# Phi of q in the buffer of phi of k, a first norm tile by tile, a second norm in two parts, and a column-tiled form for the values of segment 1: one change to a scheduled two-layer kernel

## The chip, the cores and the metric

One core of a Trainium2 chip. The metric is device time in microseconds (us) of one execution; the kernel before takes 573.08 us (median of 3, from 572.8 to 573.13). Profiles give a span that is some 1.8 us shorter than the time of the same execution, since it starts with the first instruction.

The engines are called PE or TensorE (matmul), PEld (its weight loads, which overlap its matmuls), DVE (VectorE), ACT (ScalarE), POOL (GpSimd) and SP (here the queue that issues DMA). PSUM is the memory that this kernel's matmuls write, and from which ACT or DVE copies on.

## The reference

Two layers, each an attention block with a memory and a feed-forward block (FFN), both on normed input:

```python
x = x + attn(layernorm(x))      # layer 1; 2048 tokens of 640, 32 heads of 20
x = x + relu(layernorm(x) @ w1) @ w2        # 640 -> 1728 -> 640
x = x + attn(layernorm(x))      # layer 2, the same weights
x = x + relu(layernorm(x) @ w1) @ w2

def attn(x):                    # cut to what matters
    for s in range(4):          # four segments of 512 tokens
        qs, ks, vs = ...        # 512 x 20 for each head
        a_dot = softmax(qs @ ks.T * scale + causal_mask) @ vs
        a_mem = (phi(qs) @ M) / (phi(qs) @ z + 1e-6)    # phi(t) = t+1 if t>0 else exp(t)
        outs.append(g * a_mem + (1 - g) * a_dot)
        M = M + phi(ks).T @ vs
        z = z + phi(ks).sum()
    return concat(outs) @ wo
```

## The kernel before

The file does not list instructions in their order. Each piece of work is a generator ("stream"), and a list scheduler with a small model of the engines walks all streams and appends, step by step, the operation that could start first. What comes out is a fixed order of instructions on each engine, with semaphore waits. Constants of the model never reach the chip: they only decide the order, and which of ACT and DVE does a copy out of PSUM that either could do.

```python
SEM_NS = 60.0
BY_TOKEN = 2 * G                # G = 8 groups of 4 heads in a segment
...
class Sched:
    def run(self):
        while True:
            ...                 # let every stream come to its next operation
            for prio, n, st, alts, op, late in heads:
                ...             # start = max(engine free, each awaited one + SEM_NS)
                key = (round(start + late), 0.5 if op.urgent else prio, self.rank[id(st[1])], n)
                if best is None or key < best[0]:
                    best = (key, st, end, start, k, op)
            ...                 # append it to its engine's list, advance the model
```

Values (`p @ v`) come in two forms. For the first 16 groups, segments 0 and 1 of layer 1, "by token": 40 small matmuls with tokens on the output's partitions, ready to be divided. Later groups use a column-tiled form: 16 wide matmuls, four at a time on quarters of the array; the result is transposed, so it is copied to SBUF, turned by a DMA transpose, pair by pair, and divided then.

```python
def apply(n):
    ...
    if n < BY_TOKEN:
        yield from apply_by_token(n, a, s, g, pt, mk + vt)
        return
    ...
    OD, tk = yield pe(540.0, fns, mk + vt, acq=MISC, mode="cols", lag=COLS_LAG)
    te = yield evac(L, 1, ...)          # to otu, on ACT or DVE; then turn_pair, divide
```

The norm of a segment: statistics of four tiles on DVE, one power on POOL, four normed tiles, two DMA transposes. The FFN's first matmuls need all four tiles.

```python
def lnorm(s, x_tks, pool_, parts=1):
    n = 4 // parts
    for p0 in range(0, 4, n):
        for i in range(p0, p0 + n):
            tk = yield from stats(4 * s + i, w)                 # bn_stats twice, bn_aggr
        tch = yield from chain(4 * s + p0, n, aggr)             # lnU on DVE, power on POOL
        for i in range(p0, p0 + n, 2):
            ...                                                 # two normed tiles (DVE)
            tT = yield from turn(xn_sem[id(bx)], xt.ap[...], bx.ap, [t0, t1] + xt.tks)

def ln_b(a, s):                         # the norm ahead of the FFN
    xt, xtk = yield from lnorm(s, xa, XNT_B)
```

phi of k goes to a buffer `phs`, from which a DMA transpose turns it; phi of q overwrites q in its slot, which stays taken until the read of the memory:

```python
    q = STGS[sx(a, s)][:, c, n, :]
    dst, dw = (phs[:, c * L:(c + 1) * L], PHS[c // 3].tks) if n == 0 else (q, [])
```

The softmax here doesn't subtract the row's maximum and nothing guards it: scores larger than these inputs give would overflow.

## Time and profile before

573.08 us. The page of the profile, parts 1 (busy time and share of each engine), 2 (the span in 40 slices, busy tenths) and 4 (shares of the chain of waits that ended last):

```profile
PE 558.2 (98%) x5442; PEld 306.3 (54%) x5442; DVE 406.4 (71%) x1056; ACT 408.3 (72%) x519; POOL 186.3 (33%) x291
...
PE   7999999999999999999999999999999999999998
...
PEclk9999999999999999999999999999999999999999
...
PE 82%; DVE 9%; DMA 3%; ACT 3%; SPq 1%; issue 0%; POOL 0%
```

PE is busy nearly everywhere, and 82% of the chain of waits is its. But a matmul's record is longer than its turn (0.38 us for 512 columns, where the next one can start after 0.216 us), so "busy" hides waiting. The Trainium skill ("Perfetto Trace Analysis", the note at its head) calls matmul busy time a bad metric because matmuls are pipelined.

Start, from the timeline (start, duration, engine, line, operation, output<-input, and in brackets the idle time before it and what ended it):

```profile
7.45 0.17 DVE L708 TENSOR_SCALAR mv<-asum 128x2 f32<-128x2 f32 x1 [1.67 <-ACT hT L705]
7.52 0.80 DVE L655 TENSOR_SCALAR xn_tok<-x_sb,mv,rstd 128x640 bf16<-128x640 bf16 x2
...
10.08 0.27 PE L590 MATMUL ps<-xnT,wk_r 128*128 128x256 bf16 x1 [1.25 <-ACT xnT L685]
...
19.96 1.94 ACT L1113 ACTIVATE PT<-ps 128x1024 bf16<-128x1024 f32 x2 [1.69 <-PE ps L1051]
```

DVE waited 1.67 us for ACT ahead of the norm; the first projection is at 10.08 us, the first exponential at 19.96.

Busy time by stage (the stretch, its length, then busy us and instructions of PE, PEld, DVE, ACT, POOL; granted PE clock, DMA share, GB/s):

```profile
core 0: us, PE busy (x) PEld busy (x) DVE busy (x) ACT busy (x) POOL busy (x), PEclk, DMA share, GB/s
40.00:80.00 40.00, 37.17 (x527) 19.68 (x524) 36.72 (x96) 38.39 (x46) 20.44 (x31) 1.00 0.87 201
80.00:100.00 20.00, 20.00 (x257) 11.29 (x255) 19.45 (x58) 17.50 (x23) 7.89 (x12) 1.00 0.75 143
```

In 40 to 80 us ACT is busy 38.4 of 40 us and DVE 36.7: PE depends on them there.

The two forms of values in PE's timeline:

```profile
90.18 1.17 PE L1184 MATMUL ps<-v_aug,PT 128*128 128x21 bf16 x40
91.20 0.81 PE L593 MATMUL ps<-hT,wk_r 128*128 128x512 bf16 x3
...
133.94 0.72 PE L1145 MATMUL ps<-PT,v_aug 128*21 128x512 bf16 x16
134.60 0.31 PE L593 MATMUL ps<-wo_r,oT 128*128 128x320 bf16 x1
```

By token, the next matmul starts 1.02 us later; column-tiled, 0.66 us later.

The output of segment 0 of layer 1 is turned (on SP) for the output projection, and some time later the first FFN matmul runs:

```profile
70.98 3.05 SPq L621 DMA_TRANSPOSE oT<-o_sb  x2
```

```profile
100.27 0.38 PE L590 MATMUL ps<-xnT,w_r 128*128 128x512 bf16 x1
```

### The profile page before, as it was taken

Reading aid. Unit: us, or ns where it says so; the run is one execution under the profiler, and the core shown is the slowest. Engines: PE = TensorE matmul, PEld = TensorE weight load, DVE = VectorE, ACT = ScalarE, POOL = GpSimd, SP = SyncE. Lnnn points to the kernel's source line nnn. Section 1 sums busy time; section 2 is a strip of 40 time slices with the busy share of each in tenths; the row PEclk is TensorE's granted clock in tenths of the full one; section 3 lists DMA queues with packets and bytes.
Section 4 is the critical chain, followed back from the end, with each engine's and each line's share of the span. In section 5 each row is a group of like instructions: output and inputs, shape, how many; then the busy total and the mean of one; then the engine's idle time right before and its main releaser. Section 6 shows DMA issues by size and latency. Waiting matters only on the chain.

```text
span 571.0 us, 13253 instructions
## 1 busy us (share of the span) xinstructions
PE 558.2 (98%) x5442; PEld 306.3 (54%) x5442; DVE 406.4 (71%) x1056; ACT 408.3 (72%) x519; POOL 186.3 (33%) x291
## 2 busy tenths in 40 slices
PE   7999999999999999999999999999999999999998
PEld 6664555455555543663446544465445643665655
DVE  4768999998889787879577996689747864561202
ACT  5599998987896778878768788777867778213140
POOL 4236434343434343434313443034421533100000
PEclk9999999999999999999999999999999999999999
DMA  8587997573461715843159131791419411423101
GB/s 265 89 222 163 228 186 133 156 202 57 86 171 45 111 20 153 161 66 62 23 148 185 30 65 38 179 145 22 77 42 193 109 42 20 93 65 43 51 0 47
DMA packets 125741, 59.90 MB, mean 105 GB/s; under 512 B 104562, under 2 KB 115570, under 8 KB 125682
## 3 DMA queue, kind: packets, MB, share of 16 engines
q1 hardware_dynamic: 125552, 58.90, 47.5%
q8 instruction: 43, 0.70, 0.5%
q10 hardware_dynamic: 130, 0.16, 0.2%
q14 instruction: 16, 0.13, 0.1%
HBM read 20.57 MB, written 12.85 MB: 59 GB/s over the span
## 4 chain that ended last, share of the span: by engine, by line
PE 82%; DVE 9%; DMA 3%; ACT 3%; SPq 1%; issue 0%; POOL 0%
PE ps L593 53%; PE ps L590 11%; PE ps L1051 8%; PE ps L1145 5%; PE ps L1184 2%; ACT PT L1113 2%; DVE stats L601 2%; PE ps L943 1%; PE ps L994 1%; DVE xn_tok L643 1%; DMA beta_bc<-in_A_beta_dram 1%; DVE x_sb L1267 1%; PE ps L1318 1%; DMA hT<-xn_tok 1%; DMA oT<-o_sb 1%; DVE o_sb L1239 1%
## 5 line engine op out<-in xcount | busy, mean ns | idle before, releaser
L1113 ACT ACTIVATE PT<-ps 128x1024 bf16<-128x1024 f32 x320 | 309.2, 1024 | 68.5 <-PE ps L1051 67.6
L1125 POOL TENSOR_SCALAR_AFFINE_SELECT PT<-PT 128x512 bf16<-128x512 bf16 x256 | 164.9, 662 | 282.3 <-ACT PT L1113 282.3
L593 PE MATMUL ps<-w_r,hT 128*128 128x320 bf16 x768 | 121.8, 299 | 0.0
L593 PE MATMUL ps<-xnT,w_r 128*128 128x512 bf16 x416 | 115.4, 379 | 0.0
L1267 DVE TENSOR_TENSOR x_sb<-x_sb,ps 128x320 bf16<-128x320 bf16 x128 | 60.3, 479 | 74.6 <-PE ps L593 74.2
L593 PEld LDWEIGHTS ps<-w_r,hT 128*128 128x128 bf16 x768 | 73.7, 98 | 31.2 <-issue 3.5
L1051 PE MATMUL ps<-pad 20*128 20x512 bf16 (+3 forms) x1024 | 63.4, 301 | 1.3 <-ACT PT L1113 0.9
L593 PEld LDWEIGHTS ps<-xnT,w_r 128*128 128x128 bf16 x416 | 39.7, 98 | 43.7 <-issue 4.7
L1345 ACT ACTIVATE hT<-ps 128x512 bf16<-128x512 f32 x55 | 32.9, 599 | 33.7 <-PE ps L593 33.6
L601 DVE BATCH_NORM_STATS2 stats<-x_sb 128x6 f32<-128x320 bf16 x124 | 55.6, 472 | 1.8 <-DMA x_sb<-in_A_x_dram 1.5
L593 PE MATMUL ps<-wo_r,oT 128*128 128x320 bf16 x256 | 46.5, 299 | 0.0
L1051 PEld LDWEIGHTS ps<-pad 20*128 20x128 bf16 x1024 | 17.8, 92 | 49.2 <-ACT PT L1113 23.1
L1343 DVE TENSOR_SCALAR hT<-ps 128x512 bf16<-128x512 f32 x49 | 33.2, 681 | 14.2 <-PE ps L593 14.2
L766 DVE CAST stg<-ps 128x512 bf16<-128x512 f32 (+1 forms) x45 | 28.4, 630 | 20.2 <-PE ps L593 20.1
L590 PE MATMUL ps<-xnT,w_r 128*128 128x512 bf16 x104 | 39.6, 381 | 0.0
L593 PE MATMUL ps<-wv_r,xnT 128*128 128x320 bf16 x192 | 36.1, 299 | 0.0
L1155 DVE CAST otu<-ps 128x512 bf16<-128x512 f32 x39 | 26.7, 684 | 12.3 <-PE ps L1145 12.0
L593 PE MATMUL ps<-xnT,wk_r 128*128 128x512 bf16 (+1 forms) x140 | 35.1, 349 | 0.0
L1145 PE MATMUL ps<-PT,v_aug 128*21 128x512 bf16 (+3 forms) x768 | 34.7, 301 | 0.2 <-DVE hT L1343 0.2
L593 PE MATMUL ps<-xnT,wq_r 128*128 128x512 bf16 (+1 forms) x140 | 33.8, 349 | 0.0
L911 ACT ACTIVATE stg<-stg 128x512 bf16<-128x512 bf16 x50 | 30.6, 630 | 3.0 <-DVE rtmp L909 2.9
L643 DVE TENSOR_SCALAR xn_tok<-x_sb,mv,rstd 128x640 bf16<-128x640 bf16 x60 | 30.1, 536 | 2.7 <-POOL rstd L615 2.7
(112 smaller groups left out, 685.1 us busy)
## 6 DMA issues: line engine op xcount, KB each, us to landing
pad<-scr SPq DMA_DIRECT2D x124, 80.0 KB
scr<-stg SPq DMA_DIRECT2D x34, 256.0 KB, 2.6
out_dram<-x_sb SPq DMA_DIRECT2D x16, 160.0 KB, 1.8
w_r<-in_B_w_dram SPq DMA_DIRECT2D x10, 216.0 KB, 4.5
w_r<-in_B_w_dram SPq DMA_DIRECT2D x13, 160.0 KB, 2.9
x_sb<-in_A_x_dram SPq DMA_DIRECT2D x10, 160.0 KB, 2.3
scr<-w_r SPq DMA_DIRECT2D x5, 256.0 KB, 3.9
x_sb<-in_A_x_dram SPq DMA_DIRECT2D x3, 320.0 KB, 7.3
```

What stands on the lines that cost most here:

```text
L590: bk, tk = yield pe(mm_ns(n), [(lambda e, bk, a=a, b=b: e.matmul(bk.ap[:, 0:n] if len(b.shape) == 2 else bk.ap[:, 0:n].rearrange("p (i n) ...
L593: tk = yield pe(mm_ns(n), [(lambda e, k=k, a=a, b=b, bk=bk: e.matmul(bk.ap[:, 0:n] if len(b.shape) == 2 else bk.ap[:, 0:n].rearrange("p (i ...
L601: tk = yield dve(320, 1, lambda e, c2=c2: e.bn_stats(stats6[:, t % 12, c2, :], x_sb[:, t, c2 * 320:(c2 + 1) * 320]), xt)
L643: nm = lambda e, bx, t, k: e.tensor_scalar(bx.ap[:, k * D:k * D + D], x_sb[:, t + k, :], mv[:, t + k, 0:1], rstd[:, t + k:t + k + 1], ALU. ...
L911: te = yield act(512, lambda e, q=q: e.activation(q, q, ACT.Exp), [tr] + p, psum=False)
L1051: fns.append([(lambda e, z=z, j=j, hh=hh, N=N, o=o, sl=sl, q=hh % 2: e.matmul(slot.ap[:, q, o:o + N], sl.ap[32 * hh:32 * hh + DH, z, 0, 12 ...
L1113: tx = yield act(1024, lambda e, dst=dst, src=src: e.activation(dst, src, ACT.Exp, scale=SCALE), sc + pw)
L1125: tm = yield pool(600.0, lambda e, reg=reg: e.affine_select(out=reg, in_=reg, pattern=[[0, 4], [1, 128]], compare_op=ALU.is_ge, fill=0.0, ...
L1145: fns.append((lambda e, OD, j=j, hh=hh: e.matmul(OD.ap[32 * hh:32 * hh + DH + 1, 128 * j:L], VAUG[vx(a, s)][:, j, 4 * g + hh, :], pt.ap[:, ...
L1267: ta = yield dve(320, 1, lambda e: e.tensor_tensor(x_sb[:, t, 320 * hf:320 * hf + 320], x_sb[:, t, 320 * hf:320 * hf + 320], bk.ap[:, 0:32 ...
L1343: th = yield evac(512, 1, lambda e, dc=dc, bk=bk: e.tensor_scalar(hT[:, dc, :], bk.ap[:, :], 0.0, None, ALU.max), lambda e, dc=dc, bk=bk: ...
L1345: lambda e, dc=dc, bk=bk: e.activation(hT[:, dc, :], bk.ap[:, :], ACT.Relu), [tk] + HT.tks)
```

## The change

Its intent, part by part: get the first projection out sooner (four loads, statistics and power tile by tile, the mean on ACT); spend less PE time on the values of segment 1 (column form from group 8 instead of 16); free the slots of q sooner (phi of q to `phs` too); hold the norms of segments 2 and 3 back so that DVE can empty PSUM; turn the first half of the second norm while the second half is still in its statistics; load FFN weights at another pace; and let stores be a stream of their own. The scheduler's model also gets a rule that holds certain DVE instructions back while POOL is at work, and some other estimates of durations. The diff, cut to its core (cuts marked):

```diff
-BY_TOKEN = 2 * G
+BY_TOKEN = G
 ...
+            if e == "dve" and op.port and self.free["pool"] > start:
+                hold = max(hold, self.free["pool"] - start + PORT_NS)
 ...
-            for t in range(2):
-                yield from ld("sp", "x00%d" % t, 163840, lambda e, t=t: e.dma_start(x_sb[:, t, :], xs[:, t, :]))
-            yield from x_pair("x01", 2)
+            for t in range(4):
+                yield from ld(("sp", "act")[t // 2], "x0%d%d" % divmod(t, 2), 163840, lambda e, t=t: e.dma_start(
+                    x_sb[:, t, :], xs[:, t, :]))
 ...                                   # consts: most memsets, and so the load of beta, after the first norm
+            yield Need("xt", 0, 0, 1)
 ...
-            tk = yield pe(5000.0, [... k == 59) for k in range(60)], idt)
+            tk = yield pe(4600.0, [... k == 51) for k in range(52)], idt)
 ...
+            if n == 1:
+                tk = yield pool(150, lambda e: e.tensor_scalar(lnU[:, sl], mv[:, sl, 1], 1.0, LN_EPS, ALU.mult, ALU.add), tk)
 ...                                   # first_pair -> first_sums, first_one, first_tile
-            tm = yield dve(2, 1, lambda e: e.tensor_scalar(
-                mv[:, 2:4, 0:1], asum[:, 0:2][:, :, None], 1.0 / D, None, ALU.mult), ts)
+            tm = yield act(100, lambda e: e.activation(
+                mv[:, 2:4, 0:1], asum[:, 0:2][:, :, None], ACT.Copy, scale=1.0 / D), ts, psum=False)
 ...
+            if (a, s) == (0, 2):
+                yield Need("sc",2,3,1)
+            if (a, s) == (0, 3):
+                yield Need("sc",3,4,1)
 ...
-                    if n == 0 and c in (0, 3):
+                    if c in (0, 3):
+                        if n == 0 and (s > 1 or (a, s) == (1, 0)):
+                            yield Need("phi", *divmod(NSEG * a + s - 1, NSEG))
+                        if n == 1:
+                            yield Need("turned", a, s, c // 3)
                         yield Acq([PHS[c // 3]])
-                    dst, dw = (phs[:, c * L:(c + 1) * L], PHS[c // 3].tks) if n == 0 else (q, [])
+                    dst, dw = phs[:, c * L:(c + 1) * L], PHS[c // 3].tks
 ...
-            xt, xtk = yield from lnorm(s, xa, XNT_B)
+            xt, xtk = yield from lnorm(s, xa, XNT_B, parts=2)
 ...                                   # stores, weight loads in halves, streams
```

More of the change, by code (lines that the diff above doesn't have):

```diff
@@ L110, with __init__ @@
 class Op:
-    def __init__(self, alts, waits, dma=None, acq=None, urgent=False, take=(), mode="full", lag=0.0):
+    def __init__(self, alts, waits, dma=None, acq=None, urgent=False, take=(), mode="full", lag=0.0, port=False):
         self.lag = lag
+        self.port = port
         self.alts = alts
@@ L290, in run @@
                 raise RuntimeError("stuck: " + "; ".join(
-                    str(getattr(st[2], "key", None) or [s.name for s in st[2].slots][:2]) for st in stuck))
+                    str(getattr(st[2], "key", None) or [s.name for s in getattr(st[2], "slots", [])][:2]) for st in stuck))
             _, st, end, start, k, op = best
@@ L329, in mm_ns, with dve @@
     return max(26.0, n / 2.4 + 2.6)
-def dve(n, mode, fn, waits=(), extra=0.0, acq=None, urgent=False):
-    return Op([("dve", 66.0 + n / (0.96 * mode) + extra, [(fn, True)], 95.0)], waits, acq=acq, urgent=urgent)
+PORT_NS = 150.0
+def dve(n, mode, fn, waits=(), extra=0.0, acq=None, urgent=False, port=False):
+    return Op([("dve", 66.0 + n / (0.96 * mode) + extra, [(fn, True)], 95.0)], waits, acq=acq, urgent=urgent,
+              port=port or mode > 1)
 def act(n, fn, waits=(), psum=True):
-    return Op([("act", (52.0 if psum else 94.0) + n / 1.2, [(fn, True)], 125.0)], waits)
+    return Op([("act", (60.0 if psum else 94.0) + n / 1.2, [(fn, True)], 125.0)], waits)
 def evac(n, mode, vfn, afn, waits=(), psum=True):
-    return Op([("act", (52.0 if psum else 94.0) + n / 1.2, [(afn, True)], 125.0),
+    return Op([("act", (60.0 if psum else 94.0) + n / 1.2, [(afn, True)], 125.0),
                ("dve", 66.0 + n / (0.96 * mode), [(vfn, True)], 95.0)], waits, urgent=True)
@@ L449, in ld @@
         def ld(e, name, nbytes, fn, waits=()):
-            tk = yield dma(e, sem_("d_" + name), nbytes, fn, waits, lat=2200.0)
+            tk = yield dma(e, sem_("d_" + name), nbytes, fn, waits, lat=1550.0 if name[:2] == "x0" else 2000.0)
             S.set(name, tks=[tk])
@@ L489, in half @@
                 cs = slice(h * (DFF // 2), (h + 1) * (DFF // 2))
-                return ("w1", 221184, lambda e: e.dma_start(w1_r[:, k, cs], B_w1[128 * k:128 * k + 128, cs]))
+                return ("w1%d" % h, 221184, lambda e: e.dma_start(w1_r[:, k, cs], B_w1[128 * k:128 * k + 128, cs]))
             pieces = x_pieces(2)
@@ L494, in late_loads @@
             pieces += x_pieces(3)
-            pieces += [half(k, h) for k in range(FC) for h in range(2)]
+            pieces += [half(k, h) for h in range(2) for k in range(FC)]
             n2 = len(pieces)
@@ L507, in late_loads @@
                     sems[name] = sem_("d_" + name)
-                w = yield Need("ex", *divmod(n, 5))
+                w = yield Need("ex", *divmod(25 + (n - n2) // 2 if n >= n2 else n * 19 // n2, 5))
                 if n == n2:
@@ L518, in consts @@
         def consts():
+            tw = yield dve(4, 1, lambda e: e.memset(warm[:], 0.0))
+            yield act(4, lambda e: e.activation(warm[:], warm[:], ACT.Exp), [tw], psum=False)
+            t0 = yield pool(150, lambda e: e.memset(ident[:], 0.0))
+            t1 = yield pool(250, lambda e: e.affine_select(
+                out=ident[:], in_=ident[:], compare_op=ALU.not_equal, fill=1.0, base=0,
+                pattern=[[-1, 128]], channel_multiplier=1), [t0])
+            S.set("ident", tks=[t1])
+            th = yield pool(100, lambda e: e.memset(mhalf[:], -0.5))
+            S.set("mhalf", tks=[th])
+            yield Need("xt", 0, 0, 1)
             tv = []
@@ L529, in consts @@
             S.set("z1", tks=[za, zb])
-            ta = yield dve(4, 1, lambda e: e.memset(warm[:], 0.0))
-            yield act(4, lambda e: e.activation(warm[:], warm[:], ACT.Exp), [ta], psum=False)
-            t0 = yield pool(150, lambda e: e.memset(ident[:], 0.0))
-            t1 = yield pool(250, lambda e: e.affine_select(
-                out=ident[:], in_=ident[:], compare_op=ALU.not_equal, fill=1.0, base=0,
-                pattern=[[-1, 128]], channel_multiplier=1), [t0])
-            S.set("ident", tks=[t1])
-            th = yield pool(100, lambda e: e.memset(mhalf[:], -0.5))
-            S.set("mhalf", tks=[th])
             t3 = yield pool(700, lambda e: e.memset(maskg[:], 1.0))
@@ L574, in warm_pe @@
             yield Acq([X])
-            tk = yield pe(5000.0, [(lambda e: e.matmul(
-                ps[:, 0, 0:128], ident[:], ident[:], start=True, stop=True), k == 59) for k in range(60)], idt)
+            tk = yield pe(4600.0, [(lambda e: e.matmul(
+                ps[:, 0, 0:128], ident[:], ident[:], start=True, stop=True), k == 51) for k in range(52)], idt)
             X.release(tk)
@@ L602, in stats @@
                     stats6[:, t % 12, c2, :], x_sb[:, t, c2 * 320:(c2 + 1) * 320]), xt)
-            tk = yield dve(12, 1, lambda e: e.bn_aggr(
+            tk = yield dve(50, 1, lambda e: e.bn_aggr(
                 mv[:, t, :], stats6[:, t % 12, :, :].rearrange("p c s -> p (c s)")), [tk])
@@ L609, in chain @@
             sl = slice(t0, t0 + n)
-            if sq is None:
-                tk = yield dve(n, 1, lambda e: e.tensor_scalar(lnU[:, sl], mv[:, sl, 1], LN_EPS, None, ALU.add), tk)
+            if n == 1:
+                tk = yield pool(150, lambda e: e.tensor_scalar(lnU[:, sl], mv[:, sl, 1], 1.0, LN_EPS, ALU.mult, ALU.add), tk)
+            elif sq is None:
+                tk = yield dve(n, 1, lambda e: e.tensor_scalar(lnU[:, sl], mv[:, sl, 1], LN_EPS, None, ALU.add), tk, port=True)
             else:
@@ L614, in chain @@
             h = yield Need("mhalf")
-            tk = yield pool(1000, lambda e: e.tensor_tensor(rstd[:, sl], lnU[:, sl], mhalf[:, 0:n], ALU.pow), [tk] + h)
+            tk = yield pool(740, lambda e: e.tensor_tensor(rstd[:, sl], lnU[:, sl], mhalf[:, 0:n], ALU.pow), [tk] + h)
             return tk
@@ L657, in normed @@
                 ALU.subtract, ALU.mult), [tch], extra=120)
-        def first_pair(p, tch):
-            idt = yield Need("ident")
-            if p == 0:
-                xt = yield Acq(XNT_A)
-                xt.users = []
-                S.set("xts", 0, 0, tks=[xt])
-            else:
-                xt = yield Need("xts", 0, 0)
-                xt = xt[0]
-            bx = yield Acq(XN)
-            done = []
-            tns = []
-            for k in range(2):
-                tn = yield normed(2 * p + k, k, bx, tch)
-                tns.append(tn)
-            for k in range(2):
-                t = 2 * p + k
-                tn = tns[k]
-                pb = lambda bk: bk.ap.bitcast(dt.bfloat16)
-                fns = [(lambda e, bk, c=c, k=k: e.transpose(
-                    pb(bk)[:, c * 128:(c + 1) * 128], bx.ap[:, k * D + c * 128:k * D + c * 128 + 128], ident[:]),
-                    c == FC - 1) for c in range(FC)]
-                bk, tT = yield pe(56.0 * FC, fns, [tn] + idt, acq=MISC)
-                dst = xt.ap[:, t * FC:(t + 1) * FC, :].rearrange("p c n -> p (c n)")
-                src = pb(bk)[:, 0:D]
-                tc = yield evac(D, 1, lambda e, dst=dst, src=src: e.tensor_copy(dst, src),
-                                lambda e, dst=dst, src=src: e.activation(dst, src, ACT.Copy), [tT])
-                bk.release(tc)
-                done.append(tc)
-            bx.release(tT)
-            S.set("xt", 0, 0, p, tks=done)
@@ L691, in first_ln_a, with first_tile @@
-        def first_ln_a():
-            aggr = []
+        def first_tile(t, bx, tch):
+            xt = yield Need("xts", 0, 0)
+            xt = xt[0]
+            k = t % 2
+            tn = yield normed(t, k, bx, tch)
+            idt = yield Need("ident")
+            pb = lambda bk: bk.ap.bitcast(dt.bfloat16)
+            fns = [(lambda e, bk, c=c: e.transpose(
+                pb(bk)[:, c * 128:(c + 1) * 128], bx.ap[:, k * D + c * 128:k * D + c * 128 + 128], ident[:]),
+                c == FC - 1) for c in range(FC)]
+            bk, tT = yield pe(56.0 * FC, fns, [tn] + idt, acq=MISC)
+            dst = xt.ap[:, t * FC:(t + 1) * FC, :].rearrange("p c n -> p (c n)")
+            src = pb(bk)[:, 0:D]
+            if t < 2:
+                tc = yield dve(D, 2, lambda e: e.tensor_copy(dst, src), [tT])
+            else:
+                tc = yield evac(D, 2, lambda e: e.tensor_copy(dst, src), lambda e: e.activation(dst, src, ACT.Copy), [tT])
+            bk.release(tc)
+            FIRST.setdefault(t // 2, []).append((tc, tT))
+            if len(FIRST[t // 2]) == 2:
+                bx.release(*[x for _, x in FIRST[t // 2]])
+                S.set("xt", 0, 0, t // 2, tks=[x for x, _ in FIRST[t // 2]])
@@ L693, in first_ln_a, with first_sums @@
+        FIRST = {}
+        def first_sums():
+            xt = yield Acq(XNT_A)
+            xt.users = []
+            S.set("xts", 0, 0, tks=[xt])
+            bx = yield Acq(XN)
+            S.set("bx", 0, tks=[bx])
             for t in range(2):
@@ L695, in first_ln_a, with first_one @@
                 tk = yield from stats(t, w)
-                aggr.append(tk)
-            tch = yield from chain(0, 2, aggr)
-            yield from first_pair(0, tch)
+                tch = yield from chain(t, 1, [tk])
+                S.set("first", t, tks=[tch])
+        def first_one(t):
+            bx = yield Need("bx", t // 2)
+            tch = yield Need("first", t)
+            yield from first_tile(t, bx[0], tch[-1])
         def first_ln_b():
-            w = yield Need("x01")
             junk = hT[:, 10:13, :].rearrange("p c n -> p (c n)")
@@ L704, in first_ln_b @@
             for t in (2, 3):
-                tk = yield act(D, lambda e, t=t: e.activation(
+                w = yield Need("x01%d" % (t - 2))
+                tk = yield act(D + 130, lambda e, t=t: e.activation(
                     junk[:, (t - 2) * D:(t - 1) * D], x_sb[:, t, :], ACT.Copy, accum_out=asum[:, t - 2:t - 1]), w, psum=False)
                 ts.append(tk)
-            tm = yield dve(2, 1, lambda e: e.tensor_scalar(
-                mv[:, 2:4, 0:1], asum[:, 0:2][:, :, None], 1.0 / D, None, ALU.mult), ts)
+            tm = yield act(100, lambda e: e.activation(
+                mv[:, 2:4, 0:1], asum[:, 0:2][:, :, None], ACT.Copy, scale=1.0 / D), ts, psum=False)
             ts = []
             for t in (2, 3):
-                tk = yield act(D, lambda e, t=t: e.activation(
+                tk = yield act(D + 250, lambda e, t=t: e.activation(
                     junk[:, (t - 2) * D:(t - 1) * D], x_sb[:, t, :], ACT.Square, scale=-1.0, bias=mv[:, t, 0:1],
@@ L716, in first_ln_b @@
             tch = yield from chain(2, 2, ts, sq=asum[:, 2:4])
-            yield from first_pair(1, tch)
+            bx = yield Acq(XN)
+            S.set("bx", 1, tks=[bx])
+            S.set("first", 2, tks=[tch])
+            S.set("first", 3, tks=[tch])
         def proj_ln(a, s):
@@ L770, in proj_part @@
             ev.append(te)
-            if len(ev) == (2 if (a, s) == (0, 0) else 1):
+            if len(ev) == (1 if h is None else 2):
                 S.set("stg", a, s, c, n, tks=ev)
@@ L776, in proj_first @@
             order = [(c, n, h) for h in range(2) for c in range(2) for n in range(2)]
-            order += [(c, n, h) for c in range(2, FC) for h in range(2) for n in range(2)]
+            order += [(c, n, None) for c in range(2, FC) for n in range(2)]
             for c, n, h in order:
@@ L915, in f @@
                     done.append(tp)
+                    STG[sx(a, s)][n][c].release(tp)
+                    if sx(a, s):
+                        early_done.append(tp)
                     if n == 0:
-                        STG[sx(a, s)][0][c].release(tp)
-                        if sx(a, s):
-                            early_done.append(tp)
                         if c in (2, 4):
@@ L924, in f @@
                     S.set("phi", a, s, tks=done)
+                    if sx(a, s):
+                        S.set("q01", tks=done)
             return f
@@ L944, in f @@
                             bk.ap[:, (h0 - 16 * hb) * 21:(h1 - 16 * hb) * 21],
-                            STGS[sx(a, s)][:, c, 1, i * 128:(i + 1) * 128],
+                            phs[:, c * L + i * 128:c * L + (i + 1) * 128],
                             BD[:, CH_OFF[c] + (h0 - CH_H0[c]) * 21:CH_OFF[c] + (h1 - CH_H0[c]) * 21],
                             start=(z == 0), stop=True, skip_group_check=True), z == len(lst) - 1))
-                    bk, tk = yield pe(60.0 * len(lst), fns, phi + bdt, acq=MISC[:1])
+                    bk, tk = yield pe(60.0 * len(lst), fns, phi + bdt, acq=MISC if (a, s) == (0, 1) else MISC[:1])
                     rm = yield Acq(RMEM[hb])
@@ L962, in f @@
                 if len(READ[a, s]) == 2:
-                    for c in range(FC):
-                        STG[sx(a, s)][1][c].release(*READ[a, s])
-                    if sx(a, s):
-                        S.set("q01", tks=READ[a, s])
+                    for p in range(2):
+                        PHS[p].release(*READ[a, s])
                     BDS.release(*READ[a, s])
@@ L971, in turn_k @@
             if s == NSEG - 1:
+                for p in range(2):
+                    S.set("turned", a, s, p)
                 return
@@ L977, in turn_k @@
                 PHS[p].release(tT)
+                S.set("turned", a, s, p)
                 S.set("phkT", a, s, p, tks=[tT])
@@ L1198, in apply_by_token @@
             tg = yield dve(16, 1, lambda e: e.tensor_tensor(
-                rv[:, :, :, 0], rv[:, :, :, 0], omg[:, g:g + 1].to_broadcast([128, NJ, 4]), ALU.mult), [tr] + og)
+                rv[:, :, :, 0], rv[:, :, :, 0], omg[:, g:g + 1].to_broadcast([128, NJ, 4]), ALU.mult), [tr] + og, port=True)
             dst = o_sb[:, :, 80 * g:80 * g + 80].rearrange("p i (hh e) -> p i hh e", hh=4)
@@ L1234, in divide @@
             tg = yield dve(32, 1, lambda e: e.tensor_tensor(
-                rw, rw, omg[:, 2 * q:2 * q + 2][:, :, None, :].to_broadcast([128, 2, NJ, 4]), ALU.mult), [tr] + og)
+                rw, rw, omg[:, 2 * q:2 * q + 2][:, :, None, :].to_broadcast([128, 2, NJ, 4]), ALU.mult), [tr] + og, port=True)
             tos = []
@@ L1312, in ffn_rest @@
             yield Need("hT", b, s)
-            w1t = yield Need("w1")
+            w1t = yield Need("w11")
             fns = []
@@ L1336, in ffn @@
             S.set("hT", b, s)
-            w1t = yield Need("w1")
+            w1t = yield Need("w10")
             hr = []
@@ L1340, in ffn @@
             for dc in range(NFULL):
+                if 128 * (dc + 1) > DFF // 2 >= 128 * dc:
+                    w1t = yield Need("w11")
                 bk, tk = yield from group(MISC, L, [
@@ L1352, in ffn @@
             hrest = yield Need("hR", b, s)
-            final = b == 1
             for i in range(NJ):
@@ L1364, in ffn, with store, each @@
                 S.set("xB", b, s, i, tks=tks)
-                if final:
-                    to = yield dma("sp", dout, 163840, lambda e, t=t: e.dma_start(
-                        out[0, t * 128:(t + 1) * 128, :], x_sb[:, t, :]), tks)
-                    S.last = to
             HT.release(tk)
+        def store(b, s):
+            if b == 0:
+                return
+            for i in range(NJ):
+                t = 4 * s + i
+                tks = yield Need("xB", b, s, i)
+                S.last = yield dma("sp", dout, 163840, lambda e, t=t: e.dma_start(
+                    out[0, t * 128:(t + 1) * 128, :], x_sb[:, t, :]), tks)
         dout = sem_("d_out")
         AS = [(a, s) for a in range(2) for s in range(NSEG)]
-        def each(f):
+        def each(f, early=None, late=None):
             def g():
@@ L1377, in g @@
                     S.rank[id(me)] = NSEG * a + s
+                    if early is not None:
+                        for st in S.streams:
+                            if st[1] is me:
+                                st[0] = early if (a, s) < (0, 2) else late
                     yield from f(a, s)
@@ L1405, in bass_interleave_layers__memory_aug_infini_attn__dense_activation_relu__prompt_kernel @@
         S.add(4, each(mem_write))
-        S.add(5, first_ln_a())
+        S.add(5, first_sums())
+        for t in range(TT // NSEG):
+            S.add(5, first_one(t))
         S.add(5, first_ln_b())
@@ L1414, in bass_interleave_layers__memory_aug_infini_attn__dense_activation_relu__prompt_kernel @@
         S.add(5, each(ffn_rest))
+        S.add(6, each(store))
         S.add(7, warm_pe())
```

## The prediction

> **What bounds the kernel now.** TensorE. The chain of waits gives it 82% of the span, the page has it busy 98% (558 of 571 us). The Trainium skill ("Perfetto Trace Analysis", on roofline) warns that matmul busy time is a poor measure, so I counted matmuls by shape and gave each the spacing that the timeline shows (14 of 128x320 start in 1.90 us; 40 small by-token ones take 1.02 us; 16 column-tiled ones 0.66 us; one round of scores 0.33 us). My estimate of that work is about 531 us. Of the other 40 us, about 10 pass before the first projection (10.08 us in the timeline; 60 warm-up matmuls run there and show as busy), 2.6 after the last matmul (568.3: add and store), and the rest lies mostly between 20 and 90 us plus small gaps later. In 40-80 us by windows ACT is busy 38.4 of 40 us and DVE 36.7: there TensorE waits for PSUM to be emptied. From 500 to 568 us TensorE is packed; nothing done there can help.
>
> **What changes, and its worth.**
> 1. Start. Now the normed tiles 0 and 1 start at 7.52 us although rstd was ready at 6.58: DVE sits behind an instruction that waited 1.67 us for ACT. Tile by tile, the mean on ACT, the copies on DVE: first projection near 8.5 us instead of 10.1. The second half needs the same ACT sums (two of 0.9, two of 1.0 us, then pow 0.7, norm, transposes, copy), and its tiles come on ACT's queue behind the table load, so it gains less. First exponential (19.96 us) earlier by 0.5 to 1.5 us. Worth 1 us.
> 2. Segment 1 of layer 1 (8 groups) changes from by-token values, 1.02 us of TensorE each, to the column form, 0.66: 8 x 0.36 = 2.9 us, on the critical engine. Price: an evacuation (0.60 on ACT or 0.68 on DVE) and a division of 1.67 us per pair instead of 1.04 per group, so about 0.5 us of DVE/ACT per group, 4 us, in 75-125 us where DVE is over 90% busy; and four more 3 us transposes. Net 2 us.
> 3. phi(q) into the shared buffer: same durations (0.49 against 0.47 us), no work removed. Slots of q come free after phi instead of after the memory read, and the w2 loads (now from 115 us) can start earlier. But phi(k) of the next segment now waits for the memory read, phi(q) for the transpose of phi(k): one serial chain, an estimated 25-45 us per segment against a period near 60. Should fit; worth -1 to +1 us.
> 4. Norms of segments 2 and 3 held back, faster weight loads: lets the saturated DVE empty PSUM sooner in 40-80 us. Worth 1 to 2 us.
> 5. Second norm in two parts: first half turned earlier, one more pow (0.7) on an idle POOL. Worth 0.5 us, in 80-100 us only.
> 6. Stores as a stream, 8 warm-up matmuls fewer: nothing; the tail keeps its 2.6 us.
>
> Sum: about 6 us. **Predicted 567.0 us, 8 times in 10 between 561.5 and 571.5.** Faster by over 2% (under 561.6): 0.12; within 2%: 0.86; slower: 0.02.
>
> **What would show it.** First projection at 8-9 us, first exponential at 18.5-19.5; by-token matmuls 320 instead of 640, column-tiled 896 instead of 768; the last-norm-to-end stretch unchanged in length, shifted by some 6 us; DVE busy in total slightly up; oT of segment 0 in the queue's timeline earlier than 70.98 us.
>
> **What would make it wrong.** The shared buffer's chain lasting longer than the period: memory reads late, oT late, ACT's exponentials then waiting. Or the early stage gaining more than I think: if FFN work becomes available 5 us or more sooner, under 561 is possible. If the extra DVE work at 75-125 us delays PSUM, item 2 gives nothing.

## More of the kernel before

In 80 to 100 us PE has no free time by its records.

## The result, and the profile after

569.34 us (median of 4, from 568.45 to 569.96), beside 572.94 us of the kernel before in the same rounds. The ratio of the two is 0.9936, with a 95% interval from 0.9919 to 0.9953. Ratios here are the mean time of one kernel's fast runs over that of the other's of the same rounds, so not quite the ratio of the medians. The time lies in the predicted range, and the gain is 3.6 us where 6 were forecast.

The same lines of the page, after:

```profile
PE 555.0 (98%) x5212; PEld 297.3 (52%) x5212; DVE 409.1 (72%) x1049; ACT 412.4 (73%) x527; POOL 192.1 (34%) x302
...
PE   7999998999999999999999999999999999999998
...
PEclk9999998999999999999999999999999999999999
...
PE 80%; DVE 11%; DMA 5%; ACT 2%; SPq 1%; issue 1%; POOL 0%
```

PE and its weight loads have less to do; DVE and ACT have slightly more, as forecast. In the clock row there is now an 8. The groups of instructions that belong to the two forms of values (count, busy us, mean ns):

```profile
L1172 PE MATMUL ps<-PT,v_aug 128*21 128x128 bf16 (+3 forms) x896 | 40.5, 301 | 0.0
...
L1211 PE MATMUL ps<-w_r,PT 128*128 128x21 bf16 x320 | 9.5, 172 | 0.1
```

896 and 320, as forecast. The start (the timeline again):

```profile
8.22 0.28 PE L598 MATMUL ps<-xnT,wk_r 128*128 128x256 bf16 x1 [0.59 <-DVE xnT L684]
...
18.07 0.40 PE L1078 MATMUL ps<-pad 20*128 20x512 bf16 x4
...
19.28 0.23 ACT L563 ACTIVATE gt<-beta_bc 128x32 f32<-128x32 bf16 x1 [1.22 <-DMA beta_bc<-in_A_beta_dram]
...
19.42 1.92 ACT L1140 ACTIVATE PT<-ps 128x1024 bf16<-128x1024 f32 x2
```

The first projection comes at 8.22 us (forecast: 8.5), the first exponential at 19.42 (forecast: 18.5 to 19.5). Its scores are there 1.5 us earlier than before, at 18.07, but ACT stands idle for 1.22 us until the load of beta is in, which the change issues later. The output of segment 0 is turned at 65.63 us instead of 70.98:

```profile
65.63 3.53 SPq L631 DMA_TRANSPOSE oT<-o_sb  x2
```

The stages:

```profile
40.00:80.00 40.00, 38.60 (x510) 21.56 (x511) 32.03 (x92) 35.62 (x45) 17.99 (x28) 1.00 0.80 192
80.00:100.00 20.00, 17.63 (x160) 6.91 (x153) 15.73 (x38) 17.67 (x24) 8.84 (x13) 0.91 0.82 164
```

Compare 80 to 100 us with the table of before: PE's weight loads are busy 6.91 us instead of 11.29, and the granted clock is 0.91. Some of the difference is the form of values (by-token groups have 40 weight loads each, column-tiled ones 16), but not all. PE's own timeline shows a hole:

```profile
92.91 0.40 PE L1078 MATMUL ps<-pad 20*128 20x384 bf16 x8
95.36 0.73 PE L1345 MATMUL ps<-xnT,w_r 128*32 128x256 bf16 x20 [2.05 <-DMA xnT<-xn_tok]
```

and the stretches around it, with the columns of the stages:

```profile
93.30:95.36 2.06, 0.01 (x3) 0.00 (x0) 1.14 (x3) 2.06 (x3) 0.26 (x1) 1.00 0.77 224
95.36:96.40 1.04, 1.03 (x22) 0.65 (x23) 0.00 (x0) 0.29 (x2) 0.94 (x2) 1.00 1.06 388
96.40:99.80 3.40, 3.40 (x13) 0.92 (x11) 1.32 (x3) 2.73 (x5) 0.36 (x2) 0.50 0.87 193
```

PE has nothing to do from 93.31 to 95.36 us: the first FFN matmul (L1345) waits for a DMA transpose of normed tiles. Then comes a stretch of 3.4 us at half clock, in which 13 matmuls of PE are on record. The Trainium skill ("TensorE: Matmul & The Clock Gate", part 1, on what is happening) tells of a gate that halves PE's clock after an idle window of about 3.4 us. The trace agrees with the half, and the half-clock stretch lasts 3.41 us (96.42 to 99.83). But the 3.41 us before it were not idle: the hole is 2.05 us long, and PE's records cover 1.36 us:

```profile
93.01:96.42 3.41, 1.36 (x30) 0.67 (x27) 1.43 (x4) 2.66 (x4) 1.50 (x3) 1.00 0.85 255
```

Why the transpose is late: the second half of the second norm of segment 0 stood behind other work.

```profile
87.36 0.52 DVE L621 TENSOR_SCALAR lnU<-mv 128x2 f32<-128x2 f32 x1
...
88.34 0.81 DVE L653 TENSOR_SCALAR xn_tok<-x_sb,mv,rstd 128x640 bf16<-128x640 bf16 x2
88.41 0.77 POOL L625 TENSOR_TENSOR rstd<-lnU,mhalf 128x2 f32<-128x2 f32 x1
...
89.17 3.99 SPq L631 DMA_TRANSPOSE xnT<-xn_tok  x2
...
90.00 1.11 DVE L653 TENSOR_SCALAR xn_tok<-x_sb,mv,rstd 128x640 bf16<-128x640 bf16 x2
```

Its lnU is at 87.36 us, though its statistics were ready at 86.1, and its power on POOL comes at 88.41. By the recorded order of the scheduler, the normed tiles at 88.34 and the first of the two transposes at 89.17 are those of segment 3's attention, not needed yet; the pair at 90.00 is the FFN's, and its transpose is the second in SP's row. (The names in the trace do not tell the two apart; stall_off below, which moves them, bears it out.)

### What decides the span: the work left at 120 us

I counted for every run how much PE work was still to be done at 120 us. This is an estimate from the trace: each full matmul counts with its measured spacing (216 ns with 512 columns, 136 ns with 320, a line through these two for others, 25 ns for the 21-column ones), tiled ones with a quarter; warm-up excluded. The sum of a run is 504.4 us with 16 by-token groups and 500.7 us with 8. (The forecast's 531 had the overhead of tiled rounds in it.)

| kernel | span of the profile | work left at 120 us | (span - 120) / left | first FFN matmul at |
|---|---|---|---|---|
| before | 571.0 | 409.2 | 1.102 | 100.3 |
| changed | 568.2 | 406.7 | 1.102 | 95.4 |

The second part of the kernel runs at the same pace in both. By this count the change saves 3.7 us of PE work in all, but by 120 us it has done 1.2 us less, so 2.5 us less are left, and 2.5 x 1.10 = 2.8 us is the difference of the spans. The question of the experiments is therefore what the first 120 us are made of.

### The profile page after: what moved, and what is told of

It is laid out like the page before. It is cut to its first block, busy times and chain, and to the rows that moved or that the text cites. A ratio compares the mean times of both kernels' runs of the same rounds, so it can differ in the third digit from the quotient of the medians.

```text
span 568.2 us, 12813 instructions
## 1 busy us (share of the span) xinstructions
PE 555.0 (98%) x5212; PEld 297.3 (52%) x5212; DVE 409.1 (72%) x1049; ACT 412.4 (73%) x527; POOL 192.1 (34%) x302
## 4 chain that ended last, share of the span: by engine, by line
PE 80%; DVE 11%; DMA 5%; ACT 2%; SPq 1%; issue 1%; POOL 0%
PE ps L601 52%; PE ps L598 11%; PE ps L1078 7%; PE ps L1172 5%; DMA otk<-otu 2%; PE ps L969 1%; DVE stats L609 1%; ACT PT L1140 1%; PE ps L1211 1%; DVE xn_tok L653 1%; PE ps L1021 1%; PE ps L1345 1%; DMA oT<-o_sb 1%; DVE otu L1182 1%; DMA pad<-scr 1%; DVE phs L936 1%
## 5 line engine op out<-in xcount | busy, mean ns | idle before, releaser
L1152 POOL TENSOR_SCALAR_AFFINE_SELECT PT<-PT 128x512 bf16<-128x512 bf16 x256 | 166.6, 668 | 271.7 <-ACT PT L1140 271.7
L1182 DVE CAST otu<-ps 128x512 bf16<-128x512 f32 x47 | 32.3, 687 | 15.2 <-PE ps L1172 15.0
L1172 PE MATMUL ps<-PT,v_aug 128*21 128x128 bf16 (+3 forms) x896 | 40.5, 301 | 0.0
L625 POOL TENSOR_TENSOR rstd<-lnU,mhalf 128x2 f32<-128x2 f32 (+2 forms) x26 | 20.6, 791 | 47.2 <-DVE lnU L621 45.0
```

The lines of the kernel that those rows point to most:

```text
L1152: tm = yield pool(600.0, lambda e, reg=reg: e.affine_select(out=reg, in_=reg, pattern=[[0, 4], [1, 128]], compare_op=ALU.is_ge, fill=0.0, ...
L1172: fns.append((lambda e, OD, j=j, hh=hh: e.matmul(OD.ap[32 * hh:32 * hh + DH + 1, 128 * j:L], VAUG[vx(a, s)][:, j, 4 * g + hh, :], pt.ap[:, ...
L1182: te = yield evac(L, 1, lambda e: e.tensor_copy(dst, OD.ap), lambda e: e.activation(dst, OD.ap, ACT.Copy), [tk] + OTU[0].tks)
```

## The experiments

A "draw" below is one order that the list scheduler happens to make for a kernel. Theories at the start. A: the column form's saved PE work is the gain, as predicted, and the hole at 93 us eats a part of it. B: the order that the list scheduler happens to make is what counts, not the parts. C: the column form brings nothing, its DVE and ACT work eats it; the start and the shared buffer bring the gain. Later D was added: the changed parts move the early stage as such.

Three of the runs ("replay") are made so that B cannot disturb them: the order that the scheduler chose for the changed kernel was recorded, 5058 steps, and is replayed instead of being searched; then single entries are moved. Replayed without a move it gives the same instructions in the same order on every engine. The edit that they share:

```diff
-            heads = []
-            ...                        # the search for the best head
+            st, k = self.streams[CH.index(ORDER[self.step]) // 2], CH.index(ORDER[self.step]) % 2
+            self.step += 1
+            ...
+            best = (None, st, end, start, k, op)
```

All results. Time is the median; the ratio is against the kernel before in the same rounds:

| run | time | ratio, 95% interval | span | work left at 120 us | first FFN matmul at |
|---|---|---|---|---|---|
| changed | 569.34 | 0.9936, 0.9919 to 0.9953 | 568.2 | 406.7 | 95.4 |
| tok_only | 573.88 | 1.0008, 0.9989 to 1.0028 | 571.9 | 408.5 | 101.6 |
| tok_undone | 569.24 | 0.9925, 0.9907 to 0.9944 | 567.5 | 406.2 | 93.8 |
| stall_off (replay) | 567.49 | 0.9908, 0.9876 to 0.9939 | 565.4 | 405.5 | 94.2 |
| beta_early (replay) | 569.64 | 0.9930, 0.9906 to 0.9953 | 568.2 | 406.9 | 95.7 |
| late_start (replay) | 568.56 | 0.9918, 0.9899 to 0.9936 | 567.4 | 406.7 | 97.0 |
| phi_undone | 573.32 | 1.0007, 0.9992 to 1.0022 | 572.5 | 410.9 | 101.4 |
| lnb_one | 568.98 | 0.9929, 0.9914 to 0.9944 | 568.0 | 406.2 | 94.0 |
| sem62 | 573.75 | 1.0013, 0.9993 to 1.0033 | 571.1 | 409.7 | 99.2 |
| sem58 | 570.33 | 0.9956, 0.9917 to 0.9996 | 566.1 | 405.3 | 94.8 |
| sem70 | 571.66 | 0.9975, 0.9953 to 0.9997 | 570.1 | 409.3 | 98.2 |
| bsem58 | 573.25 | 1.0001, 0.9976 to 1.0026 | 572.0 | 410.9 | 100.0 |
| bsem62 | 574.00 | 1.0021, 0.9992 to 1.0049 | 571.0 | 410.0 | 99.6 |

All were correct. The kernel before was at 572.8 to 572.9 us in every job.

### tok_only and tok_undone: the column form by itself, and taken out

In the kernel before (tok_only), and reversed in the changed kernel (tok_undone):

```diff
-BY_TOKEN = 2 * G
+BY_TOKEN = G
```

> The kernel before with one constant of the change: segment 1 of layer 1 in the column form. Theory A (the gain is TensorE work): 320 fewer and 128 column-tiled matmuls more, 2.9 us less on TensorE, so 569.5 to 571 us. Theory B (what counts is the order that the list scheduler makes anew, not the part): anything from 570 to 575 us. Theory C (column form brings nothing, its DVE and ACT work eats the gain; the start and the shared buffer bring it): 572 to 574 us.

> The changed kernel with segment 1 put back to by-token values, all else of the change kept. Theory A: about 572 us, 2.9 above the changed kernel. Theory B: 568 to 573, no relation to the part. Theory C: within 0.7 us of the changed kernel, 569 to 570.

tok_only was 573.88 us, no gain; tok_undone 569.24, no loss. Both forecasts of theory A failed: the saved PE time does not reach the end in either direction. The trace of tok_only shows where it goes. In the kernel before PE has no wait on record from 80 to 100 us; here it stands idle for 1.9 us of them, and among its waits is one of 1.06 us for DVE to copy the column form out of PSUM (`otu`):

```profile
80.00:100.00 20.00, 18.09 (x184) 8.51 (x182) 19.49 (x52) 17.89 (x23) 8.84 (x13) 1.00 0.73 173
...
97.04 0.40 PE L1051 MATMUL ps<-pad 20*128 20x384 bf16 x8 [0.84 <-ACT PT L1113]
...
99.15 0.34 PE L943 MATMUL ps<-BD,w_r 128*128 128x147 bf16 x3 [1.06 <-DVE otu L1155]
```

The changed kernel has its hole there. The same stage of tok_undone, with by-token values:

```profile
80.00:100.00 20.00, 20.00 (x257) 10.30 (x256) 18.00 (x48) 17.68 (x22) 8.83 (x13) 1.00 0.77 173
```

There is no hole and no lowered clock: PE goes on to the first FFN matmul, earlier than in the changed kernel, without waiting for it:

```profile
93.85 0.38 PE L598 MATMUL ps<-xnT,w_r 128*128 128x512 bf16 x1
```

By 120 us tok_undone has done 98.2 us of work and the changed kernel 94.0: 4.2 us more, which is a little more than the 3.7 us that its other form adds in all. So in this pair of orders the by-token matmuls ran in time that otherwise stands empty. PE is the busiest engine of the whole run, yet in this stage its time was not what was short. And the column form needs its evacuation, its transpose and its division: the output of segment 1 is turned at 128.7 us in tok_undone and at 138.6 us in the changed kernel. That difference stands in every order: 127.4 to 130.4 us in the four kernels with by-token values, 135.1 to 141.2 in the ten with the column form.

The times are weaker evidence. Each of these kernels was scheduled anew, so the sizes are only as good as the draws below allow, and a weaker form of A is not excluded: stall_off, next, has the column form without the hole and is 1.8 us under tok_undone, in another order and with one slow run of four.

### stall_off: the hole closed

```diff
 replayed order of the changed kernel, DVE:
+ lnU<-mv                  (second half of the FFN's norm)
  rtmp<-w_r
  otu<-ps
  stg<-ps
- lnU<-mv
+ xn_tok<-x_sb x2          (the FFN's)
  M_sb<-M_sb,ps
- xn_tok<-x_sb x2          (segment 3's)
  stg<-ps
  phs<-w_r,rtmp
- xn_tok<-x_sb x2          (the FFN's)
+ xn_tok<-x_sb x2          (segment 3's)
 POOL: the power ahead of two masks; SP: the FFN's transpose first, segment 3's behind one copy
```

> The changed kernel with its own order recorded and replayed, with eight entries moved: the second half of the second norm of segment 0 no longer stands behind three DVE instructions, two mask instructions and the norm and transpose of segment 3. The order of TensorE and ACT is the same, instruction by instruction. Theory A: the first FFN matmul comes near 92.5 us instead of 95.4, the TensorE clock does not drop at 96 us, and of the 3 us of idle time and 1.7 us of half clock at least 3 us reach the end: 565 to 566.5 us. Theory B or C, or if exponentials bind after 97 us: 568.5 to 569.5 us.

567.49 us, the best of all; one of its four runs took 570.57 (mean clock 0.994 over that run), the other three 566.8 to 567.8 (1.000). The hole is gone, and PE no longer waits for that transpose:

```profile
93.86 0.40 PE L1078 MATMUL ps<-pad 20*128 20x384 bf16 x8
94.19 0.73 PE L1345 MATMUL ps<-xnT,w_r 128*32 128x256 bf16 x20
```

```profile
80.00:100.00 20.00, 18.16 (x188) 7.51 (x184) 16.70 (x42) 18.22 (x25) 10.08 (x13) 1.00 0.87 169
```

The clock is at 1.00 in the stage. The span is 565.4 instead of 568.2 us. That is less than the 3 us asked for as the least, and it came from 94.19 us, not 92.5: the FFN's place in PE's order is behind the last projections, and there it soon meets scores that wait for exponentials. The interval of its ratio overlaps that of the changed kernel, so the 1.8 us between the medians are likely but not proved; that it beats the kernel before is clear.

### beta_early and late_start: does the start reach the end?

```diff
 loads():
             yield from x_pair("x11", 6)
+            yield from ld("sp", "beta", 16384, lambda e: e.dma_start(beta_bc[:], ...))
 consts():
-            yield Need("x11")
-            tb = yield dma("sp", sem_("d_beta"), 16384, lambda e: e.dma_start(...))
+            tb = (yield Need("beta"))[0]
```

> The changed kernel with its own order replayed and one entry moved: the load of beta right behind the loads of segment 1 instead of behind four copies. The first exponential no longer waits for it: near 18.3 us instead of 19.42. If a start that is earlier for ACT reaches the end (theory A in its first step), 0.5 to 1 us faster: 568.3 to 568.8. If the early stage absorbs it: 569.3 as the changed kernel.

The first exponential came at 18.78 us (near 18.3 was expected), 0.64 earlier, and no longer behind a load:

```profile
18.55 0.23 ACT L563 ACTIVATE gt<-beta_bc 128x32 f32<-128x32 bf16 x1 [0.19 <-issue]
18.78 1.02 ACT L1140 ACTIVATE PT<-ps 128x1024 bf16<-128x1024 f32 x1
```

569.64 us: absorbed. The other way:

```diff
-            tk = yield pe(4600.0, [... k == 51) for k in range(52)], idt)
+            tk = yield pe(6500.0, [... k == 84) for k in range(85)], idt)
```

> The changed kernel with its own order replayed and 85 warm-up matmuls instead of 52: TensorE's first transpose comes about 1.8 us later, near 7.9 us, so the first projection comes near 9.8 to 10.1 us as in the kernel before. If the earlier start is a part of the gain: 1.3 to 1.9 us slower than the changed kernel, 570.6 to 571.2. If it is absorbed (the exponentials or the stall at 93 us take it up): under 0.6 us slower.

The first projection came at 9.50 us, 1.28 later (9.8 to 10.1 was expected):

```profile
9.50 0.28 PE L598 MATMUL ps<-xnT,wk_r 128*128 128x256 bf16 x1 [0.70 <-DVE xnT L684]
```

568.56 us: not slower, even with PE's order the same to the instruction. The first FFN matmul is 1.6 us later too (97.0), but PE arrives at it later as well, the hole shrinks to 1.33 us, the clock does not drop, and at 120 us 406.7 us are left, the same as in the changed kernel.

```profile
97.00 0.73 PE L1345 MATMUL ps<-xnT,w_r 128*32 128x256 bf16 x20 [1.33 <-DMA xnT<-xn_tok]
```

So the earlier start is real, and on balance worth nothing in this order: it ends in the hole. On balance, because two things moved at once. The half-clock stretch that fell away is worth up to 1.7 us of PE time (half of 3.41), so it may have paid for a cost of the late start; no run separates the two.

### phi_undone and lnb_one: two more parts taken out

phi_undone takes back the four hunks of phi of q (with them the PSUM buffers that segment 1's read of the memory may use), lnb_one one argument:

```diff
 phi_undone (cut: with it go the waits for "phi" and "turned" and the release of slots after phi):
-                    dst, dw = phs[:, c * L:(c + 1) * L], PHS[c // 3].tks
+                    dst, dw = (phs[:, c * L:(c + 1) * L], PHS[c // 3].tks) if n == 0 else (q, [])
 ...
-                            phs[:, c * L + i * 128:c * L + (i + 1) * 128],
+                            STGS[sx(a, s)][:, c, 1, i * 128:(i + 1) * 128],
 lnb_one:
-            xt, xtk = yield from lnorm(s, xa, XNT_B, parts=2)
+            xt, xtk = yield from lnorm(s, xa, XNT_B)
```

> The changed kernel with phi of q back in its own slots, all else kept. As predicted before (part worth -1 to +1 us): 568 to 571. If the shared buffer is what makes the rest possible: 572 or more. The order is made anew, so a difference under about 1.5 us says nothing by itself.

> The changed kernel with the second norm in one part again. Theory A: the stall before the first FFN stays or grows, since both transposes come at the end: 569 to 571.5. If the two parts are worth nothing: 569 to 570.

lnb_one: 568.98 us, no loss; its first FFN matmul is even earlier (94.0). phi_undone: 573.32, the whole gain gone, its first FFN matmul at 101.4 us. Taken alone this would make the shared buffer the cause. The next run warns against it.

### sem62, sem58, sem70, bsem58, bsem62: the same kernels in other orders

```diff
-SEM_NS = 60.0
+SEM_NS = 62.0        # sem62, bsem62; 58.0 in sem58, bsem58; 70.0 in sem70
```

In the changed kernel (sem) and the kernel before (bsem). The work is the same, but not only its order moves: the scheduler also chooses anew between ACT and DVE for copies out of PSUM. In sem62, DVE has 1061 instructions and ACT 515, in the changed kernel 1049 and 527; in the other draws 1 to 10 moved. The expectations below say "the same instructions", which is not quite so.

> The changed kernel with one constant of its scheduler's own model changed from 60 to 62 ns: the same instructions in another order, nothing physical. Theory B: moves by 1 us or more either way, as much as the parts do. Theory A: within 1 us of the changed kernel, unless the stall at 93 us goes or another comes, which the TensorE clock and the idle time by stage would show.

sem62 was 573.75 us: 2 ns in the scheduler's model cost 4.4 us, more than the 3.6 that the whole change had gained. Its hole, at the same place, is worse: scores wait for exponentials, values wait for a mask, and only then comes the FFN.

```profile
94.57 0.40 PE L1078 MATMUL ps<-pad 20*128 20x384 bf16 x8
97.11 0.39 PE L1078 MATMUL ps<-pad 20*128 20x512 bf16 x4 [2.14 <-ACT PT L1140]
98.58 0.72 PE L1172 MATMUL ps<-PT,v_aug 128*21 128x512 bf16 x16 [1.08 <-POOL PT L1152]
99.17 0.85 PE L1345 MATMUL ps<-xnT,w_r 128*32 128x256 bf16 x20
```

So a re-scheduled kernel that differs by some us says little about the part. To see how wide this is, both kernels were drawn again:

> The kernel before with the model constant of its scheduler at 58 instead of 60 ns: same instructions, another order. The runs so far leave two theories. B: what the change gained is one draw of an order; then orders of the kernel before scatter as widely as those of the changed one (which fell from 569.3 to 573.8 us by such a draw), and this one lies anywhere from 569 to 577. D: the changed parts move the early stage as such (first FFN matmul 5 us sooner); then this one stays at 572 to 574 with its first FFN matmul at 99 us or later.

> The same with 62 ns, the exact counterpart of the draw of the changed kernel that lost its gain. B: 569 to 577 us. D: 572 to 574 us, first FFN matmul at 99 us or later.

> The changed kernel with 58 ns. B: 568 to 575 us, wherever the first FFN matmul falls: under 98 us goes with 567 to 570, over 99 us with 573 to 575. D: 568 to 570 us, the draw with 62 being the exception.

> The changed kernel with 70 ns, a third draw. Expected as for the draw with 58: B 568 to 575 us, D 568 to 570 us. In either case TensorE work still to do at 120 us of 406 to 407 us goes with 567 to 570 us in all, 409 to 411 with 573 to 575.

The three orders of the kernel before lie from 572.9 to 574.0 us, the four of the changed kernel from 569.3 to 573.8. Neither B nor D holds as it was put. Against B: the changed kernel's draws are faster on average, 571.3 against 573.4, a difference of 2.1 us (standard error about 1 us, from this scatter, so likely and not shown). Against D: they scatter by 4.4 us, so 62 was no exception, and the changed kernel as given is the best of the four. The expectation about work left was coarse: 409.3 us (sem70) went with 571.7, not with 573 to 575, and 405.3 us (sem58) with 570.3; but sem58's runs scatter by 5 us (567.9 to 573.3), and its profile is of the quickest, with a span of 566.1. Compared span by span it holds.

The granted clock, which the record gives for each run, goes with this scatter. One half-clock stretch lowers a run's mean clock by 0.003. The kernel before has none in its 21 runs in these jobs. Over the 16 runs of the changed kernel's four draws, one run without a stretch took 567.9 us; eight with one, 568.5 to 571.8; six with two (0.994), 571.5 to 574.4; one with three (0.991), 575.1. So the half clock goes with the loss even between runs of one kernel (sem58), and phi_undone too has two or three stretches in every run. As one stretch is worth up to 1.7 us, the clock can be a large part of what a draw costs. How much is the clock itself and how much the waits that come before it was not separated.

Over the 14 kernels the span of the profile follows the work left at 120 us with a correlation of 0.95, and the ratio (span - 120) / left is between 1.098 and 1.106. Most of what a variant changes shows in the first 120 us; the spread of the ratio is still worth about 3 us of span.

## Why the prediction was right or wrong

The time was right: 569.3 in the range from 561.5 to 571.5, and "within 2%". The sum of 6 us was too large by 2.4, and it was put together from the wrong terms. In part the hit is luck: the same change in two other orders, sem62 (573.75) and sem70 (571.66), would have missed the range.

1. Start, "worth 1 us": the size of the step was right (8.22 us against the 8.5 predicted), its worth was not. late_start shows 0 on balance with the order of PE's work unchanged. The start only brings PE sooner to a stage where it waits for others.
2. Column form, "8 x 0.36 = 2.9 us, on the critical engine", net 2: this is the step that failed. The matmuls went as counted, but in 80 to 125 us the critical engine was not critical in the orders that ran, and the saved time stood empty: 573.9 us instead of at most 571 (tok_only), 569.2 instead of about 572 (tok_undone). The prediction's own warning, that the extra work might make item 2 give nothing, is what happened; whether the DVE and ACT work or the 10 us later output of segment 1 matters more was not separated.
3. Shared buffer, "-1 to +1 us": open. phi_undone lost 4.0 us, but a mere new order loses up to 4.4. PE's longest waits from 20 to 130 us in the changed kernel (2.1 us for normed tiles, then 1 us or less for exponentials, q and k) name no read of the memory, so the feared late chain is not seen.
4. Norms held back, weight loads, "1 to 2 us": not tested alone. What is left for items 3, 4 and the model's new rule together is the early stage: segment 0's output turned at 65.6 instead of 71.0 us, FFN work available 4.9 us sooner. With by-token values kept (tok_undone), 2.9 us more work is done by 120 us than in the kernel before, with the same total. In that order, this is where the gain lies, and the prediction had it only under "what would make it wrong"; phi_undone and the slow draws lose it, so it hangs on the order too.
5. Second norm in two parts, "0.5 us": 0 by lnb_one, within the scatter of orders.
6. Stores, tail: right. From the start of the last matmul to the end it is 3.0 us in both spans (568.0 to 571.0, and 565.15 to 568.2), 2.8 us earlier instead of the 6 forecast.

The estimate of where PE loses time was sound in kind (20 to 90 us) but was not asked the right question: not how much PE work a part removes, but whether PE would have had other work ready at that moment.

What stays open: which of items 3 and 4 moves the early stage, and how much of the 3.6 us is the draw. The average of the draws puts about 2.1 us on the parts and the rest on the order, with four and three draws only.

## What to carry to other kernels

Before crediting removed work on the busiest engine, look at what that engine would do next in that very stage: if its next input is not there yet, removed work turns into a wait, and with PE perhaps into a halved clock as well. In a kernel whose order a scheduler makes, first draw the order a few times with a change that leaves the work as it is, and look at each draw's clock; here that scatter (4.4 us) was larger than the change under study, and single-part comparisons without a replayed order could not be read. A recorded order with a few entries moved is the cleaner experiment, and it also found the fastest kernel, 567.5 us.

## What the Trainium skill lacked or had wrong

- "TensorE: Matmul & The Clock Gate", part 1 (half clock after an idle window of about 3.4 us) and "Why this matters for your kernels" (no gaps over about 3 us). Here the half clock came after a hole of 2.05 us (1.36 of 3.41 us busy), and in beta_early after 3.41 us in which PE was busy 2.53 us, with no single wait above 0.88 us (the columns of the stages again):

```profile
51.54:54.95 3.41, 2.53 (x61) 1.43 (x60) 2.25 (x8) 3.41 (x5) 2.46 (x4) 1.00 0.61 167
54.95:58.36 3.41, 3.41 (x11) 0.88 (x12) 2.12 (x5) 2.70 (x4) 2.09 (x4) 0.50 1.04 229
```

  How much idle time it takes is open: late_start's hole of 1.33 us was not followed by a drop. The page's section on a second failure mode has the clock swing after short idles between groups of matmuls, but gives no length for them. The clock records do fit the page's free-running window: in beta_early the two stretches start at 54.95 and 95.91 us, 40.96 us or 12 times 3.41 apart.
- The same page, on the back-to-back issue gap, gives about 131 ns for each 512-column matmul in a sustained stream with weight loads and says that the isolated formula (columns / 2.4 GHz + 2.5 ns) over-counts there. Here the formula held: five 512-column matmuls took 1.08 us, 216 ns each, and fourteen of 320 columns 1.90 us, 136 ns each, all with their own weight loads. Part 1 of the page has this figure too (215.7 ns back to back), so it is the page's 131 ns that the runs do not bear out.
- No page tells that a list-scheduled order is itself a source of scatter: 2 ns in the scheduler's model moved the time of the same work by 4.4 us.
